# Linear attention ahead of an MLP: other feature layout, denominators from extra feature columns, smaller matmul tiles

## The chip, the cores and the metric

The kernel runs on one core of one Trainium2 chip. The metric is the device time of one execution in microseconds. A core has TensorE (PE, matmuls; its weight loads are shown apart as PEld), VectorE (DVE), ScalarE (ACT), GpSimd (POOL) and SyncE (SP), each with its own instruction queue, and 16 DMA engines. Matmuls write to PSUM, which has 8 banks of 512 fp32 columns in 128 partitions; only VectorE and ScalarE read it for the others.

## The reference

Inputs are q, k, v of shape (4 batches, 4 heads, 1088 tokens, 32), S1 and S2 of shape (8, 32), and the MLP's w_in (128, 2048), w_out (2048, 128), alpha (2048).

```
phi(x)  = outer(S1 x, S2 x), 8 x 8 = 64 features per token and head
kv      = sum over tokens of phi(k) v^T;   z = sum over tokens of phi(k)
attn    = (phi(q) kv) / (phi(q) . z + 1e-6)
x       = attn with the 4 heads side by side: (4 * 1088 = 4352 tokens, 128)
h       = x w_in
out     = (max(h, 0) + alpha * min(h, 0)) w_out
```

Everything comes in and leaves in fp32; the MLP runs in bf16, attention in fp32.

## The kernel before, in words

**MLP.** max(h,0) + alpha min(h,0) is (1 - alpha) relu(h) + alpha h. So the MLP is relu(x w_in) times w_a = (1 - alpha) w_out, plus x times W = w_in (alpha w_out). `w_b_f`, `w_hl` (its high and low bf16 halves) and `winT` serve to form W once (L598). Tokens go through in groups of 512 (`mlp`, L942): 16 matmuls h (L954), 16 ReLUs on ScalarE or VectorE into bf16 (`rh`, L960 and L962), 17 accumulating matmuls (L975; L972 in the last, short group), a 32x32 block transpose on VectorE (L982) and a store. There are 8.5 groups; the last batch's second half is three groups of 256: the rest tokens, 256 tokens, 256 tokens.

**Keys.** `kfeat` and `keys`: a batch has 1024 main tokens, 8 a partition, and 64 "rest" tokens that are loaded, featured and summed apart (`k_rest`). Keys are transposed, multiplied with S1 and S2 (L636), copied from PSUM (L361), and their 64 products formed by VectorE or GpSimd (L653). k'v (L706, rest L726) and z (L719, rest L733) are small fp32 matmuls; two more (L757, L766) bring them into the form that the queries need.

**Queries.** `queries` and `ratio` keep features in partitions (64 per pair of token halves) and tokens in columns. Two rounds of eight 32x64-tile matmuls give S1 q and S2 q, each repeated to 64 rows (L828; L872 for batch 0, which comes in two halves); ScalarE copies one, VectorE multiplies it with the other (L842). Eight 64x32-tile matmuls give the denominators, repeated over 32 rows, eight more the numerators (both L785). The denominators are transposed (L792), get EPS added (L798), are inverted (L799), spread by a second transpose (L801), and multiplied into the numerators (L807), which gives x in bf16. The rest tokens of all batches take the same way once (`q_rest`).

**Order.** No loop sets the order. `plan` is a list scheduler over all operations: each has engines that it may run on, a duration, latencies, a due time worked back from the MLP's pace (`T0`, `TG`) and shifted by the table `SHIFT`; PSUM banks and SBUF buffers (`classes`) are given out as it goes. It yields one fixed sequence per engine. `FIRST` holds its due times for the first loads. SP issues all loads of q, k, v and the weights in program order, then the stores; GpSimd has the key products and most of the weight work (L556). Ahead of the first group TensorE also runs matmuls without use (`dummy`, L499) to stay busy.

Of the kernel before, what the change touches and what calls it, by code (L numbers as in the profile page):

```python
# [11 lines left out]
F32 = mybir.dt.float32  # L12
# [22 lines left out]
class Op:  # L35
# [245 lines left out]
def kernel(  # L281
# [54 lines left out]

    def sb(b):
        return tiles[b.cls][b.slot]

    PK_MOST, PQ_MOST, PH_MOST = 3, 6, 4  # L340
    AW = 64
    KPE = [True, False, False, False]
# [724 lines left out]
```

## Time and profile before

| | |
|---|---|
| median of 3 runs | 113.41 us (113.07 to 113.61) |
| span of the profiled execution, first to last instruction | 110.9 us |
| between the two | 2.5 us |
| PE / PEld busy | 105.3 / 54.9 us |
| DVE / ACT / POOL busy | 83.7 / 75.5 / 24.1 us |
| DMA | 11.25 MB, mean 101 GB/s |
| first MLP matmul, last matmul ends | 15.39 us, 107.6 us |

The profile states no total of its own for the profiled execution; its span is set beside the median of the runs. Each view counts in microseconds from the span's start. "Busy" for a matmul includes its modelled pipeline, so busy times of matmuls that overlap add up to more than the clock. A row of the chain of waits is: start, length, what ran. A row in the order of time is: start, length, engine, line of the code, operation, output <- inputs, shapes, count, and in brackets the idle time before it with what ended it. A row of a group has busy time and mean length after the first bar, idle time behind the second.

### The profile page before, as it was taken

The numbers are of one execution on the slowest core, as the hardware profiler recorded it, in microseconds if no ns is written. First come the engines' busy times: TensorE is split into PE (matmuls) and PEld (weight loads), VectorE is DVE, ScalarE is ACT, GpSimd is POOL, SyncE is SP. The second block draws the span as 40 slices with busy tenths as digits, with TensorE's granted clock in tenths as the row PEclk, the third lists the DMA queues.
The fourth block names the chain that finished last, engine by engine and source line by source line (L and its number), as shares of the span: only waits on it lengthen the run. The fifth ranks groups of instructions, "written<-read, shape, count | busy, mean of one in ns | idle before, by whom it ended". The sixth has DMA issues, their size and how long they took to land.

```text
span 110.9 us, 3535 instructions
## 1 busy us (share of the span) xinstructions
PE 105.3 (95%) x1458; PEld 54.9 (50%) x1458; DVE 83.7 (75%) x157; ACT 75.5 (68%) x161; POOL 24.1 (22%) x24
## 2 busy tenths in 40 slices
PE   7999989989999989999999999999999999999980
PEld 2677333626354653447443353444534544588870
DVE  3179879999989388995667978986538798679850
ACT  2444699987689671891983963597596278797860
POOL 2040099980039008921500000000000000000000
PEclk9999999999999999999999999999999999999999
DMA  2999999779669942041002200050050005033231
GB/s 76 267 284 298 243 310 312 154 198 315 101 145 343 145 68 46 6 71 29 0 0 47 47 6 0 6 95 0 0 87 8 6 0 95 0 57 56 33 59 48
DMA packets 37536, 11.25 MB, mean 101 GB/s; under 512 B 27008, under 2 KB 37520, under 8 KB 37520
## 3 DMA queue, kind: packets, MB, share of 16 engines
q1 hardware_dynamic: 37264, 10.95, 41.9%
q8 instruction: 11, 0.18, 0.7%
q10 hardware_dynamic: 256, 0.08, 0.3%
q14 instruction: 5, 0.04, 0.2%
HBM read 8.80 MB, written 2.23 MB: 99 GB/s over the span
## 4 chain that ended last, share of the span: by engine, by line
PE 75%; SPq 8%; DMA 6%; POOL 5%; issue 2%; DVE 1%; ACT 0%; DVEq 0%
PE ps L975 26%; PE ps L954 24%; SPq L385 8%; PE ps L785 7%; PE ps L828 6%; DMA w_out_f<-in_moe_w_out_dram 6%; PE ps L636 3%; PE ps L706 3%; POOL w_b_f L556 2%; POOL w_a_bf L556 2%; PE ps L972 2%; PE ps L598 2%; POOL w_hl L556 1%; PE ps L757 1%; PE ps L726 1%
## 5 line engine op out<-in xcount | busy, mean ns | idle before, releaser
L954 PEld LDWEIGHTS <-w_in_bf 128*128 128x128 bf16 x160 | 15.0, 98 | 15.4 <-issue 3.6
L954 PE MATMUL ps<-xT__96,w_in_bf 128*128 128x512 bf16 (+1 forms) x80 | 21.5, 358 | 0.4 <-ACT rh__82 L960 0.4
L975 PEld LDWEIGHTS <-w_a_bf 128*128 128x128 bf16 x144 | 13.6, 98 | 14.4 <-issue 2.0
L954 PE MATMUL ps<-xT__97,w_in_bf 128*128 128x512 bf16 (+1 forms) x80 | 19.2, 336 | 0.0
L960 ACT ACTIVATE rh__82<-ps 128x512 bf16<-128x512 f32 (+1 forms) x22 | 12.2, 555 | 4.9 <-PE ps L954 4.7
L960 ACT ACTIVATE rh__83<-ps 128x512 bf16<-128x512 f32 (+1 forms) x22 | 11.9, 543 | 3.6 <-PE ps L954 3.6
L960 ACT ACTIVATE rh__84<-ps 128x512 bf16<-128x512 f32 (+1 forms) x16 | 8.5, 532 | 0.9 <-PE ps L954 0.6
L960 ACT ACTIVATE rh__86<-ps 128x512 bf16<-128x512 f32 (+1 forms) x15 | 8.3, 551 | 1.0 <-PE ps L975 0.5
L792 DVE STREAM_TRANSPOSE dt__78<-ps 128x1024 f32<-128x1024 f32 (+2 forms) x6 | 5.6, 937 | 3.9 <-PE ps L785 3.9
L975 PE MATMUL ps<-rh__83,w_a_bf 128*128 128x512 bf16 (+1 forms) x22 | 7.9, 359 | 0.0
L960 ACT ACTIVATE rh__85<-ps 128x512 bf16<-128x512 f32 x11 | 6.7, 605 | 0.9 <-PE ps L954 0.9
L975 PE MATMUL ps<-rh__82,w_a_bf 128*128 128x512 bf16 (+1 forms) x20 | 7.3, 363 | 0.0
L960 ACT ACTIVATE rh__87<-ps 128x512 bf16<-128x512 f32 (+1 forms) x11 | 5.8, 527 | 2.0 <-PE ps L954 1.8
L975 PE MATMUL ps<-rh__84,w_a_bf 128*128 128x512 bf16 (+1 forms) x19 | 6.8, 357 | 0.4 <-POOL w_a_bf L556 0.4
L975 PE MATMUL ps<-rh__86,w_a_bf 128*128 128x512 bf16 (+1 forms) x20 | 7.1, 353 | 0.0
L975 PE MATMUL ps<-rh__85,w_a_bf 128*128 128x512 bf16 (+1 forms) x19 | 6.8, 356 | 0.0
L828 PE MATMUL ps<-qT__74,Sab 32*64 32x512 f32 x96 | 6.7, 613 | 0.0
L982 DVE STREAM_TRANSPOSE oT__91<-ps 128x512 f32<-128x512 f32 (+1 forms) x8 | 5.4, 681 | 1.6 <-PE ps L975 1.4
L962 DVE TENSOR_SCALAR rh__85<-ps 128x256 bf16<-128x256 f32 (+1 forms) x10 | 5.3, 527 | 1.7 <-PE ps L954 1.0
L653 POOL TENSOR_TENSOR kp__70<-ab__68 128x1024 f32<-128x1024 f32 x2 | 3.9, 1952 | 9.9 <-ACT ab__68 L361 5.3
L975 PE MATMUL ps<-rh__87,w_a_bf 128*128 128x512 bf16 (+1 forms) x17 | 6.0, 355 | 0.0
L653 POOL TENSOR_TENSOR kp__70<-ab__67 128x512 f32<-128x512 f32 (+1 forms) x2 | 3.0, 1510 | 13.6 <-ACT ab__67 L361 13.6
(158 smaller groups left out, 218.9 us busy)
## 6 DMA issues: line engine op xcount, KB each, us to landing
out_dram<-oT__91 SPq DMA_DIRECT2D x28, 64.0 KB, 1.9
k<-in_k_dram SPq DMA_DIRECT2D x3, 512.0 KB, 4.7
q<-in_q_dram SPq DMA_DIRECT2D x3, 512.0 KB
v<-in_v_dram SPq DMA_DIRECT2D x12, 128.0 KB, 5.6
w_in_f<-in_moe_w_in_dram SPq DMA_DIRECT2D x2, 512.0 KB, 7.2
w_out_f<-in_moe_w_out_dram SPq DMA_DIRECT2D x2, 512.0 KB, 7.1
k<-in_k_dram SPq DMA_DIRECT2D x2, 256.0 KB, 3.0
q<-in_q_dram SPq DMA_DIRECT2D x2, 256.0 KB, 3.4
```

The source lines that it names most:

```text
L385: (nc.sync if eng == "sp" else nc.scalar).dma_start(dst, src)
L556: return lambda e: (nc.vector if e == "dve" else nc.gpsimd).tensor_tensor(out=out, in0=a, in1=b, op=what)
L636: nc.tensor.matmul(ps(bf)[lo + i:lo + i + aw, j * 64:(j + 1) * 64], sb(bT)[:, j * cnt + i:j * cnt + i + aw], S12blk.rearrange("p h c -> p ...
L653: (nc.vector if e == "dve" else nc.gpsimd).tensor_tensor(out=dst, in0=i0, in1=i1, op=ALU.mult)
L785: nc.tensor.matmul(dst, w, mv, start=True, stop=True, skip_group_check=True)
L792: nc.vector.transpose(bview(sb(dt), [[1, nn]]).rearrange("p (c n) -> p c n", c=2), ps(bd)[:, :, :ncp])
L828: nc.tensor.matmul(ps(bufs[t // 2])[64 * c:64 * c + 64, t % 2, :nf], bview(Sab[32 * t:32 * t + 32, i], [[1, R]]), moving(sb(bq), t, c), st ...
L954: nc.tensor.matmul(ps(b)[:, :n], w_in_bf[:, c * 128:(c + 1) * 128], xs(), start=True, stop=True)
L960: nc.scalar.activation(sb(br)[:, :n], ps(b)[:, :n], ACTF.Relu)
L962: nc.vector.tensor_scalar_max(sb(br)[:, :n], ps(b)[:, :n], 0.0)
L975: nc.tensor.matmul(ps(bo)[:, :n], w, y(), start=c == 0, stop=c == NC)
L982: o = op("dve", dv(n) + 40, lambda e: nc.vector.transpose(bview(sb(boT), [[1, n]]), ps(bo)[:, :n]), [last], [bo, boT], 80, end, f"oT{g}")
```

## The change

It rewrites attention's data layout and leaves the MLP as it is.

- **Tokens.** A partition now holds 34 tokens of one head (128 partitions are 4 heads x 32), so one contiguous row per partition is loaded for k and q. All 1088 tokens go one way; the loads, features and sums of the "rest" are gone. Token slots in a 32-column block are split over four column groups of 8 or 9; two of the 34 slots of each batch (64 tokens) go to a small tensor `xr`, which makes up the group of 256 that the rest tokens made up before.
- **Keys** (`key_part`). One block transpose (L604 of the new file), 8 matmuls on 64x32 tiles with S1 and S2 (L610), a transpose back (L613), products (L626) on GpSimd (VectorE helps for batch 0), k'v (L665, L670) and z (L650, L656).
- **Denominator weights.** z, as an 8x8 matrix, is masked (L679), multiplied with S1 (L682) and reduced into 8 more columns of the query weight `Wq` of its batch (L685): the denominator of a token is the dot product of S2 q with these 8 columns.
- **Queries** (`query_part`). Sixteen matmuls on 32x32 tiles (L711) give 24 features per token and head; VectorE transposes them (L717), forms the denominator as 8 products and a sum with EPS (L724, L725), inverts it (L730) and multiplies S2 q by it (L731). Then come the 64 products (L742; VectorE or GpSimd), their transposes (L745), and 32 matmuls on 32x32 tiles for the numerators (L756), which are x already; ScalarE or VectorE copies them into bf16.
- **Scheduler.** New `T0`, `TG`, `FIRST`, `SHIFT` and buffer counts. The second part of batch 0's q is now loaded after the first halves of w_in and w_out.
- **Stores** follow the new token order, again 128 B pieces, 512 B in the last.

The core of the diff (the scheduler's table and the removed functions are left out):

```diff
-    T0, TG = 14500.0, 10200.0
+    T0, TG = 13000.0, 9200.0
...
+    def load_rows(name, t, src, b, lo=0, hi=NT):
+        load(name, "sp", t[b][:, lo * D:hi * D],
+             bass.AP(tensor=src.tensor, offset=b * H * S * D + lo * D, ap=[[NT * D, 128], [1, (hi - lo) * D]]),
+             128 * (hi - lo) * D * 4)
...
+        def fe(e):
+            for hp in range(2):
+                for c in range(4):
+                    P = slice(64 * hp, 64 * hp + 64)
+                    nc.tensor.matmul(ps(pair)[32 * c:32 * c + 32, hp, :n], Wk[P].rearrange("p a b c -> p (a b c)"),
+                                     sb(bT)[P, offs[c] * D:offs[c] * D + n], start=True, stop=True, skip_group_check=True)
+        o = op("pe", n * 1.67 + 30, fe, [o, c_Wk], [bT, pair], 200, name=tag + "ab", mode=2, ni=32)
+        o = op("dve", dv(2 * n) + 35, lambda e: nc.vector.transpose(
+            at(sb(bab), 0, [[2 * r, 2 * ns], [n, 2], [1, 2 * r]]), ps(pair)[:, :, :n]), [o], [pair, bab], 80, name=tag + "abT")
...
+        o1 = op("pe", 150, lambda e: nc.tensor.matmul(ps(bz)[:, 64:96], S1sel.rearrange("p h d -> p (h d)"), sb(bt),
+                                                      start=True, stop=True, skip_group_check=True), [o1, c_sel], [bz, bt], 200,
+                name=f"zM{b}", mode=1, ni=4)
+        w_done[b] = op("dve", 110, lambda e: nc.vector.tensor_reduce(
+            out=Wq[:, b, 2 * r:3 * r], in_=at(ps(bz), 64, [[1, r], [r, 4]]), axis=AX.X, op=ALU.add), [o1, c_Wq], [bz], 80, name=f"zW{b}")
...
+        def fe(e):
+            for c in range(4):
+                for h in range(H):
+                    P = slice(32 * h, 32 * h + 32)
+                    nc.tensor.matmul(ps(f2[h // 2])[32 * c:32 * c + 32, h % 2, :n], Wq[P, b],
+                                     sb(bT)[P, offs[c] * D:offs[c] * D + n], start=True, stop=True)
+        o = op("pe", n * 1.67 + 40, fe, [o, c_Wq, w_done[b]], [bT] + f2, 200, name=tag + "f", mode=2, ni=64)
+        ot = []
+        for y in range(2):
+            def ft(e, y=y):
+                nc.vector.transpose(at(sb(bf)[:, 0], 2 * y * D, [[D, 2], [H * D, ns], [1, D]]),
+                                    ps(f2[y])[:, :, :n].rearrange("p h (s t) -> p h s t", t=D))
...
+        def den(e):
+            t = sb(bt)
+            nc.vector.tensor_mul(t[:, :m, :r], F(r, r), F(2 * r, r))
+            nc.vector.tensor_reduce(out=t[:, :m, r + 1], in_=t[:, :m, :r + 1], axis=AX.X, op=ALU.add)
...
+        def rec(e):
+            t = sb(bt)
+            nc.vector.reciprocal(t[:, :m, r + 2], t[:, :m, r + 1])
+            nc.vector.tensor_mul(F(r, r), F(r, r), at(t[:, 0], r + 2, [[12, m], [0, r]]))
...
+        def num(e):
+            for y in range(2):
+                for h in range(H):
+                    for c in range(4):
+                        P = slice(32 * c, 32 * c + 32)
+                        w = ns if c in extra else main
+                        nc.tensor.matmul(ps(n2[c // 2])[32 * h:32 * h + 32, c % 2, :w * D], kvW[b][P, y, h],
+                                         at(sb(bp)[P, 0], (2 * h + y) * D, [[2 * H * D, w], [1, D]]),
+                                         start=y == 0, stop=y == 1, skip_group_check=True)
...
-        x[b] = q_main(b, LATE) if b else q_first(LATE)
-    xr, bxr = q_rest(LATE)
+        keys(b, LATE)
+        x[b] = query_main(b) if b else query_first()
```

More of the change, by code (lines that the diff above doesn't have):

```diff
@@ L338, in sb, with at @@
         return tiles[b.cls][b.slot]
+    def at(t, x, free):
+        return bass.AP(tensor=t.tensor, offset=t.offset + x, ap=[list(t.ap[0])] + [list(d) for d in free])
     PK_MOST, PQ_MOST, PH_MOST = 3, 6, 4
-    AW = 64
-    KPE = [True, False, False, False]
     ops = []
@@ L398 @@
-    v_rs = [consts.tile([128, H, D], F32, tag=f"vr{m}", name=f"vr{m}") for m in range(2)]
-    q_rs = consts.tile([128, 2, H, D], F32, tag="qr", name="qr")
+    k_sb = [consts.tile([128, NT * D], F32, tag=f"k{b}", name=f"k{b}") for b in range(B)]
+    q_sb = [consts.tile([128, NT * D], F32, tag=f"q{b}", name=f"q{b}") for b in range(B)]
+    v_sb = [consts.tile([128, H, 9 if b else 10, D], F32, tag=f"v{b}", name=f"v{b}") for b in range(B)]
     w_in_f = consts.tile([DM, NC, 132], F32, tag="w_in_f")
@@ L458 @@
     for b in range(1, B):
[L459 to L460 removed]
+        load_rows(f"k{b}", k_sb, k, b)
+        load_rows(f"q{b}", q_sb, q, b)
         load_v(b)
[L462 to L469 removed]
     def got(name):
@@ L488, in zeros @@
         nc.vector.memset(tab, 0.0)
-    op("dve", 950, zeros, due=-1e7, name="zero")
+        nc.vector.memset(Wq, 0.0)
+        for t in tiles["tm"]:
+            nc.vector.memset(t[:, :, r:r + 1], EPS)
+    op("dve", 1150, zeros, due=-1e7, name="zero")
     c_zero = ops[-1]
@@ L658 @@
-    rest_k, rest_ab = {}, {}
-    def k_rest(m, due, i=None):
-        rows = None if i is None else (SR * i, SR)
-        P = slice(0, 128) if i is None else slice(SR * i, SR * i + SR)
-        tag = f"kr{m}" if i is None else f"kr{m}.{i}"
-        o = kfeat([k_rs[m][P].rearrange("p h d -> p (h d)")], got(tag), due,
-                  lambda: bview(ab_rest[m], [[1, 64]]), lambda: bview(kp_rest[m], [[1, 256]]),
-                  [], [], ("dve",), tag, rows=rows)
-        for b in (2 * m, 2 * m + 1) if i is None else (2 * m + i,):
-            rest_ab[b] = o[0].deps[0]
-            rest_k[b] = o + got(tag.replace("k", "v", 1))
@@ L846, in q_first, with key_part, pr @@
-    def q_first(due):
+    kvW = [consts.tile([128, 2, H, D], F32, tag=f"kvW{b}", name=f"kvW{b}") for b in range(B)]
+    kv_done = [None] * B
+    w_done = [None] * B
+    def key_part(tag, src, needs, nj, offs, ns, kp_eng, split):
+        n = ns * D
+        bT, pair, bab = Buf("kT"), pq(), Buf("ab")
+        o = op("dve", dv(nj * D) + 35, lambda e: nc.vector.transpose(sb(bT)[:, :nj * D], src), needs, [bT], 80, name=tag + "T")
+        def fe(e):
[7 more added lines that the diff above has]
+            at(sb(bab), 0, [[2 * r, 2 * ns], [n, 2], [1, 2 * r]]), ps(pair)[:, :, :n]), [o], [pair, bab], 80, name=tag + "abT")
+        if split:
+            bkp, base = [Buf("kp"), Buf("kp")], (0, 0)
+        else:
+            bkp, base = [Buf("kp")] * 2, (0, 2 * ns)
+        res = []
+        for hp in range(2):
+            def pr(e, hp=hp):
+                m = 2 * ns
+                dst = at(sb(bkp[hp]), base[hp] * R, [[R, m], [r, r], [1, r]])
+                i0 = at(sb(bab), hp * m * r, [[r, m], [1, r], [0, r]])
+                i1 = at(sb(bab), n + hp * m * r, [[r, m], [0, r], [1, r]])
+                (nc.vector if e == "dve" else nc.gpsimd).tensor_tensor(out=dst, in0=i0, in1=i1, op=ALU.mult)
+            res.append(op(kp_eng[hp], {"dve": dv(128 * ns), "pool": 110 + 128 * ns * 1.8}, pr, [o],
+                          [bab, bkp[hp]], 80, name=f"{tag}kp{hp}"))
+        return bab, n, bkp, base, o, res
@@ new lines, in half, with f @@
+            def half(y, u=u):
+                def f(e, n2):
+                    x0, step = (32, 480) if u and y == 0 else (0, 512)
+                    copy(e, sb(bx)[:, u, 256 * y:256 * y + 256].rearrange("p (c n) -> p c n", c=2),
+                         at(ps(n2[y]), x0, [[step, 2], [1, 128]]))
+                    if u:
+                        copy(e, sb(br)[:, 0, y], at(ps(n2[y]), 640 * y, [[1, D]]))
+                return (f"x{u}.{y}", (256, 32) if u else (256,), [y], [bx, br] if u else [bx], f)
@@ L918, in q_rest, with half, f @@
-    def q_rest(due):
-        bx = Buf("xT")
-        def moving(qT, t, c):
-            w = qT[32 * t:32 * t + 32].rearrange("p h j d -> p (h j d)")
-            return w[:, 128 * c:128 * c + 128]
-        def nums(a, dst):
-            for be in range(2):
-                for h in range(H):
-                    for c in range(2):
-                        yield (2 * c + be, h, c, a[64 * c:64 * c + 64, 2 * be:2 * be + 2, 32 * h:32 * h + 32],
-                               dst(h)[:, c, 64 * be:64 * be + 64])
-        def xmul(g, num, rr):
-            yield bview(sb(bx), [[1, 1024]])[:, 128 * g:128 * g + 128], num[:, g, :128], rr[:, g]
-        aq, mu = queries("qr", got("qr0") + got("qr1"), due, q_rs.rearrange("p c h d -> p (c h d)"), 128, moving)
-        return ratio("qr", aq, mu, list(range(B)), nums, 128, xmul, bx, [0, 1]), bx
+        def half(g):
+            def f(e, n2):
+                copy(e, sb(bx)[:, g].rearrange("p (c n) -> p c n", c=2), at(ps(n2[g]), 32 * g, [[512 - 32 * g, 2], [1, 256]]))
+                if g:
+                    copy(e, sb(br)[:, b], at(ps(n2[1]), 0, [[768, 2], [1, D]]))
+            return (f"x{g}", (512, 64) if g else (512,), [g], [bx, br] if g else [bx], f)
@@ new lines, in turned, with f @@
+        def turned(c):
+            def f(e, n2):
+                if c == 0:
+                    copy(e, sb(br)[:, b], at(ps(n2[1]), 0, [[768, 2], [1, D]]))
+                    copy(e, sb(bx)[:, 1, :256], ps(n2[1])[:, 0, 32:288])
+                else:
+                    copy(e, sb(bx)[:, 1, 256:].rearrange("p (t s) -> p t s", s=8), ps(n2[1])[:, 1, :256].rearrange("p (s t) -> p t s", s=8))
+            return (f"x1.{c}", (256,) if c else (64, 256), [1], [bx] if c else [bx, br], f)
+        xc = [half(0)] + ([half(1)] if b < B - 1 else [turned(0), turned(1)])
```

499 lines of the change are left out of this document (161 added, 338 removed), and 201 rows, old and new, of the table SHIFT.

## The prediction

> **What bounds the kernel now.** I read the page's first two parts for the engine that is always busy, then the chain of waits for the point from which nothing else matters, then the order in time for prices.
>
> ```profile
> span 110.9 us, 3535 instructions
> PE 105.3 (95%) x1458; PEld 54.9 (50%) x1458; DVE 83.7 (75%) x157; ACT 75.5 (68%) x161; POOL 24.1 (22%) x24
> PE   7999989989999989999999999999999999999980
> PEclk9999999999999999999999999999999999999999
> PE 75%; SPq 8%; DMA 6%; POOL 5%; issue 2%; DVE 1%; ACT 0%; DVEq 0%
> ```
>
> TensorE has work in every slice, at the full granted clock throughout, and is three quarters of the chain of waits. The chain in order of time shows where it takes over:
>
> ```profile
> 10.53 6.56 DMA w_out_f<-in_moe_w_out_dram
> 17.16 2.04 POOL w_b_f L556 x2
> 19.19 1.00 POOL w_a_bf L556
> 21.27 1.16 POOL w_hl L556
> 23.48 0.82 PE ps L975 x3
> 24.30 1.04 PE ps L828 x16
> 25.35 0.59 PE ps L785 x16
> 26.26 1.75 PE ps L598 x16
> 28.01 0.43 PE ps L954 x2
> 36.45 1.03 PE ps L706 x64
> 37.48 0.12 PE ps L719 x16
> 38.96 0.11 PE ps L626
> 63.17 1.07 PE ps L785 x16
> 106.37 1.24 PE ps L972 x22
> 107.63 0.30 DVE oT__93 L363
> ```
>
> Up to 23.5 us the chain runs over the second half of w_out (landed at 17.09) and the weight work on GpSimd. From there to 107.6 it is TensorE alone; after it come 110.9 - 107.6 = 3.3 us of copy and store. So this kernel's time is a head, a TensorE stream, and 3.3 us. The stream's first MLP matmul:
>
> ```profile
> 15.39 0.82 PE L954 MATMUL ps<-xT__96,w_in_bf 128*128 128x512 bf16 x3
> ```
>
> From 15.39 to 107.6 are 92.2 us. The MLP is 8.5 groups of 512 tokens with 33 matmuls each; two take 0.43 us, so 280.5 x 0.2155 = 60.4 us. The bf16 product of the two weights (L598) is 1.75. What is left, 30 us, is attention (with the weight transposes and under 1 us of idle). That is the part the change rewrites.
>
> **The stream after.** I list what the changed kernel puts on TensorE behind its first MLP matmul, in its own order: feature work of batches 1 to 3, and the last product of batch 0's second half. Prices are the rows above. Eight fp32 tiles with one matmul each (16 records of L785; an fp32 matmul leaves two) take 0.59 us at 256 columns and 1.07 at 512, so 1.875 ns a column and 0.11 fixed: 0.65 at 288, 0.62 at 272, 0.38 at 144.
> - Key features: 8 matmuls on 64x32 tiles, 288 columns: 0.65 x 3 = 1.95.
> - Query features with denominators: 16 matmuls on 32x32 tiles, 288 columns. If sixteen run as eight do, 0.65 x 3 = 1.95.
> - Numerators: 32 matmuls in two rounds of sixteen, on average 272 columns: 1.24 x 3 = 3.72; the half of batch 0 has 144 columns: 0.76.
> - k'v: 32 + 4 matmuls, 72 records at 1.03 / 64 = 16.1 ns: 1.16 x 3 = 3.48.
> - z: 10 matmuls, 20 records at 0.12 / 16: 0.15 x 3 = 0.45; its product with S1, taken as 0.1: 0.3; two transposes of 0.11 (the L626 row): 0.66.
>
> Together 13.3 us instead of 30. All of before's denominators, second feature product, rest keys and the rest query path are gone from the stream. With 60.4 and 1.75 unchanged the stream is 75.5 us, 16.7 less than the 92.2.
>
> **What nobody has run yet is sixteen tiles at once.** The trace has at most eight (32x64 and 64x32). The bounds are 16 at a time (6.43 us for query features and numerators) and 8 (twice that, +6.4). I take sixteen: the rows below are 32-row tiles in all four row groups, and the L706 row above has 32-column tiles in all four column groups, and both overlap.
>
> ```profile
> 24.23 1.11 PE L828 MATMUL ps<-qT__74,Sab 32*64 32x512 f32 x16
> L828 PE MATMUL ps<-qT__74,Sab x96: 587/613/639, 24.2 to 67.9; 32*64 32x512 f32 x96
> ```
>
> Sixteen records of 613 ns, 9.8 us in all, pass in 1.04 us of the chain. The Trainium skill (TensorE: Matmul & The Clock Gate, "Measured speedup vs the span model") gives 10.6 times for sixteen bf16 tiles; counted as 10.6 tiles in place of 16 that would be an estimate of 6.43 x (16/10.6 - 1) = 3.3 us more. No row here has sixteen.
>
> **The head.** GpSimd keeps ten weight operations: four on w_out's first half, then six behind the second half's landing. Before:
>
> ```profile
> 13.88 1.04 POOL L556 TENSOR_TENSOR w_b_f<-w_out_f,alphaT 128x512 f32<-128x512 f32 x1 [5.47 <-DMA w_out_f<-in_moe_w_out_dram]
> 15.87 1.16 POOL L556 TENSOR_TENSOR w_hl<-w_b_f,w_hl 128x512 bf16<-128x512 f32 x1
> 23.39 1.03 POOL L556 TENSOR_TENSOR w_b_f<-w_out_f,alphaT 128x512 f32<-128x512 f32 x1
> L653 POOL TENSOR_TENSOR kp__71<-ab__68 128x1024 f32<-128x1024 f32 x1 | 2.0, 1955 | 0.0
> ```
>
> About the same bytes go ahead of w_out's second half (3.7 MB), so I keep its 17.1; two w_b, one w_a and three w_hl after it are 2.04 + 1.00 + 3 x 1.16 = 6.5, which gives 23.7. The first half may land up to 0.9 us earlier than before (13.88), since the second q part of batch 0 is now queued behind it; if not, its four operations end at 18.0 and the six at 24.5. I take 23.9. Behind them in GpSimd's queue now stand batch 1's two key products of 1152 elements: 1152/1024 x 1.955 = 2.2 each, until 28.3. TensorE's order has batch 1's k'v, then batch 0's second numerators, ahead of the second MLP group, so it waits there: before that point it has 24 MLP matmuls, the weight product and small work, 8.5 us from its first MLP matmul. That first one needs: q0.1 landed (2.72 MB ahead and with it, as many as w_out's first half had, so 12.9 to 13.9), its transpose, the transpose of the first products, numerators, two feature transposes of q0.1 and a copy, all in VectorE's order: 0.67 + 1.15 + 0.8 + 0.6 + 0.33 and waits, 16.2 to 17.4. The sixteen first ReLUs, mostly on ScalarE at 0.49 a start, hold it until about 24; then 1.75 + 0.65 bring TensorE to 26.5. So 28.3 decides, with 1.8 us of slack for the first matmul. k'v with its wait to 29.6, numerators to 30.3. Of the 75.5, 5.2 + 0.65 + 0.15 + 0.1 + 1.75 + 0.65 + 1.16 + 0.76 = 10.4 have passed; 65.1 are left.
>
> **The other engines.** They decide whether TensorE stays fed. Starts of consecutive operations give their pace:
>
> ```profile
> 60.75 1.23 DVE L815 STREAM_TRANSPOSE qT__74<-q 128x1024 f32<-128x1024 f32 x1
> 61.91 1.18 DVE L842 TENSOR_TENSOR aq__76<-ps,aq__76 128x1024 f32<-128x1024 f32 x1
> 64.35 1.25 DVE L792 STREAM_TRANSPOSE dt__78<-ps 128x1024 f32<-128x1024 f32 x1 [0.65 <-PE ps L785]
> 65.63 0.21 DVE L798 TENSOR_SCALAR dt__78<-dt__78 128x32 f32<-128x32 f32 x1
> 65.87 0.36 DVE L799 RECIPROCAL dt__78<-dt__78 128x32 f32<-128x32 f32 x1
> 66.26 1.25 DVE L801 STREAM_TRANSPOSE rr__80<-dt__78 128x1024 f32<-128x1024 f32 x1
> L681 DVE STREAM_TRANSPOSE kT__64<-k x2: 611/620/630, 27.1 to 27.6; 128x256 f32<-128x256 f32 x2
> 20.20 0.60 ACT L960 ACTIVATE rh__85<-ps 128x512 bf16<-128x512 f32 x1
> 20.69 0.60 ACT L960 ACTIVATE rh__82<-ps 128x512 bf16<-128x512 f32 x1
> ```
>
> 1024 elements cost VectorE 1.16, and 0.12 more where the next operation needs them. Per batch it did: key transposes 4 x 0.55, q 1.16, two products 2.3, dT 1.28, add and reciprocal 0.6, rr 1.39, x 1.2: 10.1, with 0.8 for z. After: k and q transposes 1.2 each, ab 0.67, features 2 x 0.67, denominators 0.85, reciprocal and division 0.8, products 2.55 where VectorE has them (batch 2; one of two in batch 3, none in batch 1), their transposes 2.55, z 0.3: 8.9 to 11.5. So VectorE gets nothing off while the stream gets 17 us shorter. ScalarE loses two copies of 0.96 and its ab copies and gains two x copies of 0.5: about 1.4 less a batch. Until batch 1's numerators VectorE has about 18 us of work against a stream of 20 plus its waits, in the next two stages 14.3 against 21.6 and 14.4 against 14.5, so it runs ahead before the tight one. I take 1.5 us for waits in the rest: three group starts where only 0.86 to 1.08 us of other matmuls cover the copy of x (0.2 + 0.6 + 0.07), and some late ReLUs. Bounds: 0, and 4 from the second rival.
>
> **Loads and stores.** The loads of q, k, v and weights are still issued by SP; k and q rows grow from 1 KB to 4.3 KB, v rows from 256 B to 1 KB. From b = 1 on loads lie behind 60 us of stream and I give them nothing. Stores keep 128 B pieces, and the last store 512 B, so the 3.3 us tail stays.
>
> **Sum.** 30.3 + 65.1 + 1.5 = 96.9 for the last matmul, + 3.3 = 100.2 span. The median of the runs is 113.41 beside a span of 110.9; the 2.5 between them I keep: 102.7 us.
>
> **Rivals.**
> 1. Sixteen tiles run as more than eight but fewer than sixteen: 102.7 to 109.1. For it: no row shows sixteen. Against: both halves of the pattern overlap fully. The Trainium skill's figure (same section) gives 106.0, an estimate.
> 2. VectorE feeds TensorE late. L681 writes its result with a stride and pays 0.55 us for 256 elements, twice the plain price; the new ab and feature transposes write rearranged too. If they cost double, 3 x 0.57 = 1.7 us more a batch, and up to 2 more where ReLUs queue behind; 104 to 107. Against: they write whole runs of 16 or 32.
> 3. The GpSimd wait isn't there, since w_out lands earlier or the products are covered: 16.2 + 75.5 + 1.0 + 3.3 + 2.5 = 98.5.
> 4. Small records have a floor of their own, so that more tiles at once don't help. There are 96 + 256 + 48 + 216 + 60 + 6 + 12 = 694 behind the first MLP matmul; at L706's 16.1 ns they take 11.2 us, under the 13.3, and nothing changes. The Trainium skill (TensorE: Matmul & The Clock Gate, "Wait — 56ns, not 53.3ns?") has starts never under about 25 ns apart: by that rule 17.4 us, 106.8 in all, an estimate; L706's 64 records in 1.03 us disagree.
> 5. Slower: the tiles' overlap breaks down, as only one column or row group streams at a time. At w tiles at a time, query features and numerators cost 6.43 x 16/w; w = 4 gives +19.3, 122 us. It decides below w = 6, where 6.43 x (16/6 - 1) = 10.7 eats the whole gain. Against: eight overlap in L785 and L828.
>
> **How the numbers follow.** Forecast 0.60 (100 to 105 by itself); rival 1, 0.12; 2, 0.09; 3, 0.08; 4, 0.02; 5, 0.07; no measurable change (within 0.5%, about what a measurement of this kernel can tell), 0.02. That is 0.91 faster, 0.02 same, 0.07 slower. The range from 98.5 (rival 3) to 108.5 leaves out rival 5, no change, and the edges of 1 and 3, under 2 in 10.
>
> **What would show it.** Right: TensorE's attention lines behind its first MLP matmul near 13 us; 16 numerators' rounds in about 0.6 us; one idle stretch of 1 to 3 us before batch 1's k'v, ended by GpSimd; VectorE over 80% busy; the tail 3.3. Wrong: numerators near 2.4 us a batch (rival 1), TensorE idle before VectorE lines all through (2), no idle at k'v (3).

## The result and the profile after

The changed kernel takes 109.84 us, the median of four executions (107.89 to 113.08), beside 113.42 for the kernel before. The ratio is 0.959 (95% interval 0.949 to 0.969); it leaves out executions that the comparison takes for disturbed, while the medians in this document are over all. So it is faster, as forecast, but by about 4% and not by 9.5%, and 109.84 lies above the range. The profiled execution took 109.28 us: a span of 107.5 and 1.8 around it.

The page's first two parts and its chain by engine, of the kernel after:

```profile
span 107.5 us, 3290 instructions
PE 96.5 (90%) x1351; PEld 52.0 (48%) x1365; DVE 81.5 (76%) x139; ACT 72.0 (67%) x157; POOL 40.1 (37%) x30
PE   7968897796969989999999899999999999999950
DMA  2999999999998123001400140041023014051131
PE 57%; POOL 11%; DVE 10%; ACT 6%; DMA 5%; issue 4%; SPq 3%; DVEq 0%
```

TensorE is busy for eight tenths or more of every slice from the thirteenth (32 us) to the last two, as before, but the first third now has gaps, and TensorE's share of the chain fell from 75% to 57%: the head has grown, and other engines set it. While it lasts, the DMA engines are full (the 9s of the last row but one, up to 32 us). The chain in order of time:

```profile
20.58 2.28 POOL w_hl L543 x2
22.86 2.25 POOL w_a_bf L543
25.11 1.12 POOL w_hl L543
26.23 2.14 POOL kp__68 L626
28.36 2.15 POOL kp__69 L626
30.55 0.97 PE ps L665 x51
31.52 0.83 issue
33.02 1.10 PE ps L756 x37
34.28 1.03 PE ps L842 x4
42.86 1.51 PE ps L756 x41
66.81 1.70 PE ps L756 x44
```

GpSimd ends its key products at 30.5, batch 1's k'v (L665) follows at once, breaks off after 51 of its records, and goes on 0.83 us later. Batch 0's second numerators (L756) end at 34.12 and the MLP resumes at 34.28. (Those 0.16 us are most likely one MLP matmul without a record: this trace lists 1365 weight loads but only 1351 matmuls, and in the control below, with 1365 of both, the same stretch is five matmuls in 1.19 us without a gap, where here 0.16 is followed by four in 1.03. I keep 34.28.) The forecast had 30.3 for that point, 96.9 for the last matmul and 100.2 for the span; the trace has 34.28, 103.7 and 107.5. Of the 7.3 us that the span is too long, 4.0 lie ahead of that point, 2.8 behind it, and 0.5 in the tail.

### The profile page after: what moved, and what is told of

The parts are those of the page before. It is cut to its first block, busy times and chain, and to the rows that moved or that the text cites. A ratio compares the mean times of both kernels' runs of the same rounds, so it can differ in the third digit from the quotient of the medians.

```text
span 107.5 us, 3290 instructions
## 1 busy us (share of the span) xinstructions
PE 96.5 (90%) x1351; PEld 52.0 (48%) x1365; DVE 81.5 (76%) x139; ACT 72.0 (67%) x157; POOL 40.1 (37%) x30
## 4 chain that ended last, share of the span: by engine, by line
PE 57%; POOL 11%; DVE 10%; ACT 6%; DMA 5%; issue 4%; SPq 3%; DVEq 0%
PE ps L842 21%; PE ps L821 21%; PE ps L756 6%; DMA v<-in_v_dram 5%; POOL w_hl L543 3%; SPq L386 3%; POOL w_a_bf L543 2%; POOL kp__69 L626 2%; POOL kp__68 L626 2%; POOL w_b_f L543 2%; PE ps L665 2%; PE ps L711 2%; PE ps L839 2%; DVE ft__73 L731 2%; DVE ph__75 L742 1%
## 5 line engine op out<-in xcount | busy, mean ns | idle before, releaser
L821 PE MATMUL ps<-xT__94,w_in_bf 128*128 128x512 bf16 (+1 forms) x80 | 19.8, 337 | 0.3 <-DVE Wq L685 0.3
L821 PE MATMUL ps<-xT__93,w_in_bf 128*128 128x512 bf16 x62 | 19.0, 379 | 0.9 <-ACT xT__93 L365 0.5
L827 ACT ACTIVATE rh__81<-ps 128x512 bf16<-128x512 f32 (+1 forms) x22 | 12.2, 556 | 4.9 <-PE ps L821 4.8
L626 POOL TENSOR_TENSOR kp__68<-ab__66 128x1152 f32<-128x1152 f32 (+1 forms) x5 | 9.7, 1955 | 13.5 <-DVE ab__66 L613 12.9
L827 ACT ACTIVATE rh__82<-ps 128x512 bf16<-128x512 f32 (+1 forms) x20 | 11.3, 567 | 0.9 <-PE ps L821 0.8
L742 POOL TENSOR_TENSOR ph__76<-ft__73 128x1280 f32<-128x1280 f32 (+1 forms) x2 | 5.6, 2822 | 15.6 <-DVE ft__73 L731 15.6
L827 ACT ACTIVATE rh__83<-ps 128x512 bf16<-128x512 f32 (+1 forms) x18 | 9.8, 544 | 2.1 <-PE ps L656 1.0
L482 PE MATMUL ps<-const-bfloat16-1.0 128*128 128x512 bf16 x27 | 8.5, 448 | 1.1 <-PEq L911 0.8
L842 PE MATMUL ps<-rh__82,w_a_bf 128*128 128x512 bf16 (+1 forms) x22 | 7.9, 359 | 0.5 <-issue 0.5
L717 DVE STREAM_TRANSPOSE ft__73<-ps 128x576 f32<-128x576 f32 (+2 forms) x10 | 6.0, 642 | 2.7 <-PE ps L711 2.7
L827 ACT ACTIVATE rh__84<-ps 128x512 bf16<-128x512 f32 (+1 forms) x14 | 7.4, 529 | 0.9 <-PE ps L821 0.8
L827 ACT ACTIVATE rh__85<-ps 128x512 bf16<-128x512 f32 (+1 forms) x12 | 7.1, 593 | 0.2
L756 PE MATMUL ps<-pt__77,kvW 32*32 32x128 f32 (+3 forms) x320 | 7.2, 353 | 0.0
L745 DVE STREAM_TRANSPOSE pt__77<-ph__75 128x1280 f32<-128x1280 f32 (+1 forms) x5 | 6.9, 1383 | 0.1
L827 ACT ACTIVATE rh__86<-ps 128x512 bf16<-128x512 f32 (+1 forms) x10 | 5.4, 539 | 2.0 <-PE ps L821 2.0
L827 ACT ACTIVATE rh__87<-ps 128x512 bf16<-128x512 f32 (+1 forms) x12 | 6.4, 532 | 0.5 <-PE ps L821 0.2
L842 PE MATMUL ps<-rh__81,w_a_bf 128*128 128x512 bf16 (+1 forms) x19 | 6.7, 351 | 0.0
L742 DVE TENSOR_TENSOR ph__75<-ft__73 128x1280 f32<-128x1280 f32 (+1 forms) x4 | 6.6, 1640 | 0.1
```

What stands on the lines that cost most here:

```text
L482: nc.tensor.matmul(PS[:, 7], ones(128), ones(512), start=True, stop=True, skip_group_check=True)
L626: (nc.vector if e == "dve" else nc.gpsimd).tensor_tensor(out=dst, in0=i0, in1=i1, op=ALU.mult)
L717: nc.vector.transpose(at(sb(bf)[:, 0], 2 * y * D, [[D, 2], [H * D, ns], [1, D]]), ps(f2[y])[:, :, :n].rearrange("p h (s t) -> p h s t", t=D))
L742: (nc.vector if e == "dve" else nc.gpsimd).tensor_tensor(out=dst, in0=i0, in1=i1, op=ALU.mult)
L745: oT.append(op("dve", dv(k) + 35, lambda e, lo=lo, hi=hi, bph=bph: nc.vector.transpose(sb(bp)[:, lo:hi].rearrange("p a b -> p (a b)"), sb( ...
L756: nc.tensor.matmul(ps(n2[c // 2])[32 * h:32 * h + 32, c % 2, :w * D], kvW[b][P, y, h], at(sb(bp)[P, 0], (2 * h + y) * D, [[2 * H * D, w], ...
```

## The experiments

The point at which TensorE resumes the MLP behind batch 0's second numerators splits every trace below into a head and a rest. I call it the resumption.

### Single operations measured alone

A kernel of its own, without the computation: VectorE's forms alone and beside GpSimd, then rounds of small fp32 matmuls.

```diff
+ for n, f, t in ((1024, dve_ss, "ss"), (288, dve_ss, "sm"), (1024, dve_sd, "sd"), ...):   # alone
+     f(n, t); f(n, t)
+ ...
+ for i in range(m): f(n, t)            # and, at the same time,
+ for i in range(4): pool_ss(512, t)
+ ...
+ for n in (32, 64, 128, 160, 208, 256, 288, 512):        # 2 rounds on 16 tiles: 64 records
+     for y in range(2): for h in range(4): for c in range(4):
+         nc.tensor.matmul(PS[32*h:32*h+32, 2+c, :n], w[32c..], mv[32c.., 512*y:512*y+n], start=y==0, stop=y==1)
```

> This kernel leaves the whole computation out (it writes zeros) and measures single operations. Part one: GpSimd's product of 512 elements and six VectorE forms, each alone and then beside the other engine. Theory (the two engines hinder each other when both read two operands from SBUF): GpSimd 1.03 us alone and 2.0 to 2.3 beside VectorE's products with two SBUF operands; VectorE's 1024-element product 1.2 alone and 1.9 to 2.4 beside GpSimd, its 288-element product 0.46 to 1.4; nothing changes beside a product that reads PSUM, a transpose, a sum or a ReLU. Rival (the long ones of the trace come from the loads that land at that time): with no loads here, no form gets longer. Part two: rounds of 64 records on 32x32 tiles with 32 to 512 columns. Theory (records have a floor of about 16.3 ns and sixteen tiles overlap fully beyond it): 1.04 us at 32, 64 and 128 columns, 1.19 at 288, 2.0 at 512. Rival (sixteen tiles run as about thirteen): 1.04, 1.45 at 288, 2.4 at 512. Rival (eight at a time): 2.2 at 288, 3.9 at 512.

Groups of VectorE alone (dss and dsm: both operands in SBUF; dsd: one in PSUM), and GpSimd alone; mean ns behind the comma:

```profile
L63 DVE TENSOR_TENSOR dss<-za,zb 128x1024 f32<-128x1024 f32 x2 | 2.4, 1222 | 0.0
L67 DVE TENSOR_TENSOR dsd<-ps,zb 128x1024 f32<-128x1024 f32 x2 | 2.4, 1221 | 0.0
L63 DVE TENSOR_TENSOR dsm<-za,zb 128x288 f32<-128x288 f32 x2 | 0.9, 456 | 0.0
L83 POOL TENSOR_TENSOR galone<-pa,pb 128x512 f32<-128x512 f32 x3 | 3.8, 1261 | 0.2
```

The same groups with both engines at work:

```profile
L63 DVE TENSOR_TENSOR dss<-za,zb 128x1024 f32<-128x1024 f32 x5 | 10.0, 2006 | 0.1
L83 POOL TENSOR_TENSOR gss<-pa,pb 128x512 f32<-128x512 f32 x4 | 7.6, 1906 | 0.2
L63 DVE TENSOR_TENSOR dsm<-za,zb 128x288 f32<-128x288 f32 x5 | 6.2, 1239 | 0.1
L67 DVE TENSOR_TENSOR dsd<-ps,zb 128x1024 f32<-128x1024 f32 x5 | 6.1, 1223 | 0.1
L83 POOL TENSOR_TENSOR gsd<-pa,pb 128x512 f32<-128x512 f32 x4 | 5.1, 1266 | 0.2
```

Beside GpSimd, VectorE's 1024-element product grows from 1.22 to 2.01 us and its 288-element one from 0.46 to 1.24, and GpSimd's from 1.26 to 1.91 (alone it was to take the 1.03 of the kernel's rows; why it takes 1.26 here was not tried). With one operand in PSUM nothing changes, nor did it for transposes, sums and ReLUs. Since no loads land in these stretches, they are not the cause. The Trainium skill (SBUF — State Buffer, "Who interferes with whom") says that a VectorE instruction with two SBUF inputs contends with a GpSimd instruction that reads SBUF, and that the second to issue waits; these rows agree.

The rounds by their pace in the chain (L113 sixteen tiles, 64 records, at 128, 288 and 512 columns; L121 eight tiles, 32 records, at 288 and 512; L128 four tiles in one column, 16 records, at 288), all at the full clock:

```profile
72.56 1.00 PE ps L113 x56
81.27 1.53 PE ps L113 x63
83.78 2.28 PE ps L113 x62
91.96 1.13 PE ps L121 x32
94.07 1.88 PE ps L121 x32
98.47 1.10 PE ps L128 x16
```

Each set is two rounds. From 288 to 512 columns sixteen tiles take 0.75 us more, and eight also 0.75: 3.3 ns a column for both, so sixteen overlap as fully as eight. What differs is the fixed part: 1.53 - 288 x 0.00333 = 0.57 us for 64 records, against 0.17 for 32 and 0.14 for 16. None of the three theories had that: the first gave 1.19 us at 288 columns, "thirteen tiles" gave 1.45 and 2.4 and came closest by its sizes, but its reason (an incomplete overlap) is wrong. The Trainium skill's factor of 10.6 for sixteen tiles (TensorE: Matmul & The Clock Gate, "Measured speedup vs the span model"; the table does not name the data type) lies between what these rows give: set against 3.3 ns a column without a fixed part, sixteen tiles do the work of 16 x 0.96 / 1.53 = 10.0 at 288 columns and of 16 x 1.71 / 2.28 = 12.0 at 512. Its least distance of about 25 ns between starts ("Wait — 56ns, not 53.3ns?") is undercut if records are counted, 64 in 1.00 us at 128 columns or 15.6 ns each; by matmuls, of which each leaves two records, it is 31 ns, and no run here shows which of the two the figure is for.

### Order in the head: numerators first, key products first, both

In the trace TensorE has the transposes of w_in's second half (L576), which wait for its load and cast, ahead of batch 0's first numerators; and GpSimd's weight products run into VectorE's. Rows of the kernel after, in order of time:

```profile
13.11 1.22 DVE L742 TENSOR_TENSOR ph__75<-ft__73 128x1024 f32<-128x1024 f32 x1
13.17 2.06 POOL L543 TENSOR_TENSOR w_b_f<-w_out_f,alphaT 128x512 f32<-128x512 f32 x1 [1.93 <-DVE ft__73 L731]
15.19 1.03 POOL L543 TENSOR_TENSOR w_a_bf<-w_out_f,omaT 128x512 bf16<-128x512 f32 x1
17.64 0.92 PE L576 MATMUL ps<-identb,w_in_bf 128*128 128x128 bf16 x8 [0.47 <-ACT w_in_bf L365]
18.49 1.07 PE L756 MATMUL ps<-pt__77,kvW 32*32 32x128 f32 x64
20.04 1.47 PE L821 MATMUL ps<-xT__93,w_in_bf 128*128 128x512 bf16 x5 [0.49 <-ACT xT__93 L365]
21.86 2.35 DVE L742 TENSOR_TENSOR ph__75<-ft__73 128x1280 f32<-128x1280 f32 x1
22.82 2.29 POOL L543 TENSOR_TENSOR w_a_bf<-w_out_f,omaT 128x512 bf16<-128x512 f32 x1
```

The first two moves, and the next two, alone and together:

```diff
+ behind("winT1", "q0.0num", 0)      # numerators first
+ behind("winTc1", "q0.0x0.1")
+ behind("q0.1ph0", "k1abT")         # key products first
+ behind("w_a3", "k1kp0")
```

> Only TensorE's order is changed: the transposes of the input weights' second half, and their copy, go behind batch 0's first numerators, so that these and the first MLP group don't wait for that half's load and cast. Theory A (the span is set later, where batch 1's k'v waits for GpSimd's two key products): the first MLP matmul comes about 1.0 us earlier than at 20.0, k'v of batch 1 starts where it did, within 0.3 us, and the time is that of the changed kernel within 0.3 us. Theory B (the first MLP matmul sets what follows, through ScalarE's and VectorE's ReLUs): the time falls by 0.8 to 1.2 us against the changed kernel, to about 108.7 where that is at 109.7.

> Only the order on GpSimd and VectorE is changed: one weight product of GpSimd goes behind batch 1's first key product, and the product of batch 0's second query features goes behind the transpose of batch 1's key features on VectorE. Theory A (GpSimd's queue alone sets the start of batch 1's k'v): the two key products end at about 28.9 in place of 30.5 and the time falls by 1.3 to 1.6 us. Theory B (TensorE's own work, fed by the ReLUs, ends at 30.35 too, so that GpSimd is level with it): the time falls by 0 to 0.4 us, and a wait of TensorE for ReLUs or the weight product stands where that for GpSimd stood.

> Both reorderings together. If the two paths are level in the changed kernel, as the trace reads, each alone gives little and both together give 1.0 to 2.0 us more than the sum of the two alone leaves to see: 107.5 to 108.5 us. If GpSimd's queue alone decides, this equals the key-products-first kernel within 0.3 us; if the first MLP matmul alone decides, it equals the numerators-first kernel within 0.3 us.

| | first MLP matmul | k'v of batch 1 starts | resumption | span | median |
|---|---|---|---|---|---|
| after | 20.04 | 30.55 | 34.28 | 107.5 | 109.84 |
| numerators first | 19.27 | 31.04 | 33.49 | 106.5 | 110.94 |
| key products first | 20.41 | 30.82 | 33.49 | 106.9 | 110.48 |
| both | 21.26 | 32.88 | 35.55 | 108.6 | 110.41 |

None gains. Numerators first brought the first MLP matmul 0.8 us forward, but k'v came no earlier: ScalarE's copy of the moved transposes now delays its casts for GpSimd, which waits 1.0 us for them. Key products first did not end those products at 28.9: the first took 3.43 us instead of 2.17, because VectorE's moved product (2.37 us) now ran beside it. The two together were to give 107.5 to 108.5 and gave 110.41, with a median inside the spread of the others. In the profiled execution TensorE was also granted half its clock from 12 to 14 us, which I can't explain from the order, so that trace does not show what both moves would do at the full clock. Four kernels with different heads and the same median said that something else was in the way.

### The changed kernel again, and the weight product without its low half

```diff
- tt(w_b_f[:, s], w_out_f[:, s], al, ALU.mult)(e)
+ tt(w_hl[:, s, 0], w_out_f[:, s], al, ALU.mult)(e)          # straight to bf16; w_hi and w_lo go
- nc.tensor.matmul(ps(bw)[:, :2 * DM], winT[:, c], w_hl[:, c].rearrange("p y m -> p (y m)"), ...)
+ nc.tensor.matmul(ps(bw)[:, :DM], winT[:, c], w_hl[:, c, 0], ...)
```

> The changed kernel itself, unaltered, beside the reorderings below on one chip, since its executions differ by several us. Theory (what differs is when TensorE gets past batch 0's second numerators, which hangs on the landing of the loads; behind that point everything takes the same time): the span less the start of the MLP matmul behind those numerators (34.28 us of 107.5 before) is 73.0 to 73.4 us again, as in the three reordered traces (106.5 - 33.49, 106.9 - 33.49, 108.6 - 35.55), whatever the span. Rival (the stream itself varies): this difference moves by as much as the span does.

> The low half of the weight product is left out: GpSimd writes the scaled output weights straight to bf16, its four low-half subtractions and ScalarE's four casts go, and the weight product has 128 columns in place of 256. The order is that of the changed kernel. Theory A (GpSimd's queue sets the start of batch 1's k'v): GpSimd reaches the key products as soon as VectorE has batch 1's key features (24.9), both are done at about 29.2 instead of 30.5, and the time falls by 1.0 to 1.5 us. Theory B (TensorE's own path from its first MLP matmul at 20.0, paced by ScalarE, sets it): the three casts of 0.5 us between the ReLUs and 0.9 us of the weight product go, and the time falls by 1.4 to 2.4 us, with the first MLP matmul where it was. If both are level the fall is the smaller of the two, 1.0 to 1.5.

> As the one without the low half, and batch 0's first numerators ahead of the transposes of the input weights' second half on TensorE. Theory B (the first MLP matmul counts): another 0.7 to 1.0 us less than without the reordering, 2 to 3 us under the changed kernel. Theory A (GpSimd alone): no further gain, within 0.3 us.

> As the one without the low half, with both reorderings (numerators first on TensorE; on VectorE batch 1's key features ahead of the product of batch 0's second query features, on GpSimd the first key product ahead of the last weight product). Both paths are relieved at once: 3 to 4 us under the changed kernel, about 106, if the two paths are level; no better than the numerators-first form if only TensorE's path counts.

Medians: the changed kernel 110.49 (107.80 to 111.96), without the low half 110.25 (one execution at 190.8, unexplained), with numerators first 110.63, with both moves 110.50. The three expectations of a gain failed. Span less resumption was 107.9 - 34.62 = 73.3 for the changed kernel, as the theory of a constant rest had it. So time changes hands only in the head, and there the chains show the same thing at the same place. The kernel after, again:

```profile
27.80 2.15 POOL kp__69 L626
29.99 0.97 PE ps L665 x51
30.96 1.73 issue
32.69 0.42 PE ps L665 x13
34.62 1.03 PE ps L842 x4
```

Without the low half and with numerators first, where k'v starts when ScalarE's ReLUs let it:

```profile
28.29 0.50 ACT rh__88 L826
28.84 0.76 PE ps L710 x26
29.59 0.90 PE ps L664 x50
30.49 1.92 issue
34.35 1.03 PE ps L841 x4
```

TensorE breaks off after the 50th or 51st record of the same 64, and waits for nothing that the profile shows. How long does not hang on when k'v starts: 0.83 us after a start at 30.55, 1.73 after 29.99, 1.92 after 29.59, but 1.99 with both moves and no low half, where it started at 31.38. The queue called "instruction" moves blocks of 16 KB (0.16 MB in 10 packets). In the changed kernel's second trace one such packet appears in the stretch 30.0 to 30.2 us, 2.5 to 2.7 us ahead of the break's end; with numerators first and no low half in 29.8 to 30.0, 2.4 to 2.6 ahead. The five traces with a break all go on 2.4 to 3.1 us behind such a packet; the trace with numerators first alone has it at 26.8, long before k'v, and no break. The packet of the changed kernel's second trace, in the stretch 30.0 to 30.2 us:

```profile
q8 instruction: 1, 0.02, 33.1%
```

That suggested to me that TensorE runs out of instructions, whose block stands in line with the loads. That this queue is TensorE's is read from these times alone.

### The loads of later batches held back

```diff
+ hold("k3", k_sb[3][:, :1], "k1kp1")        # load k of batch 3 behind GpSimd's first key product of batch 1
+ hold("q3", q_sb[3][:, :1], "k1kp0")
+ hold("v2", v_sb[2][:, 0, 8, :1], "q1ph0")  # each by a one-column store of GpSimd into the tile
+ hold("v3", v_sb[3][:, 0, 8, :1], "q1ph1")
```

> The changed kernel, with four groups of loads held back: k and q of batch 3 until GpSimd's two key products of batch 1 are done, v of batches 2 and 3 until its two query products of batch 1 are done (a one-column store of GpSimd into the tile holds each back). Nothing else changes. Theory F (the break in the middle of batch 1's k'v, which the profile calls issue, is TensorE waiting for its next 16 KB block of instructions, whose packet is delayed by the loads): with the loads out of the way the block's packet lands before 28 us in place of 29.6 to 30.0, the break of 0.8 to 1.7 us is gone, and the median falls by 1 to 2 us, to 108.5 to 109.3; the executions spread less. Rival (the break is something of k'v's own, or the loads share nothing with it): packet, break and time stay within 0.3 us.

> The loads held back as before, and batch 0's first numerators ahead of the transposes of the input weights' second half on TensorE. Theory F: freed of the break, the earlier first MLP matmul now counts: 0.3 to 1.0 us less than with the held loads alone, 108.0 to 108.6. Rival: as the numerators-first kernel without held loads, 110.9.

> The loads held back, numerators first, and the low half of the weight product left out (GpSimd and ScalarE relieved by eight operations, the weight product by 0.9 us). Its twin without held loads broke off for 1.92 us in batch 1's k'v and resumed the MLP at 34.35. Theory F: resumes at 32.4, span 105.5, 107.3 us. Rival: 110.6 like its twin.

With the loads alone held back the median is 108.07 (ratio 0.958, 0.953 to 0.963), 1.8 to 2.4 us under the changed kernel's two medians, and five of six executions lie between 107.7 and 108.9. The ratio is no better than the changed kernel's 0.959, and the best executions are alike (107.72 here, 107.80 and 107.89 there): what changed is how often an execution comes near the best. Of executions with a granted clock of 0.99 or more, the eight of the changed kernel have spans of 105.8 to 110.0 us, the ten with the loads held back (with the control below) 105.7 to 107.1. Each run has one trace, and none of the changed kernel's best executions was profiled, so that they too break off, or don't, is not shown. The break is gone in all three traces. With numerators first the median is 110.16, a miss: GpSimd, which waits for ScalarE's casts there, ended its key products only at 33.55, in a trace that was granted half its clock from 14 to 16 us. Without the low half as well it is 108.73, not 107.3.

### The control, the query weights first, and both reliefs

```diff
+ behind("k0.1kp0", "zW0")     # VectorE: batch 0's key product behind the sum that completes the query weights
```

> The changed kernel with the loads of batches 2 and 3 held back, again, as the control for the next two on one chip: 108.1 us median, within 0.5 us.

> As the control, and VectorE's product of batch 0's keys (768 elements) goes behind the sum that completes batch 0's query weights. Theory P (that product takes 1.02 us or, beside GpSimd's, 2.09, and the query features of batch 0 wait for it in some executions, at 12.1 in place of 10.4): the features start near 10 us in every execution, the slow executions go, and the median falls by 0.3 to 1 us, to 107.1 to 107.8. Rival (the loads' landing decides the spread): no change within 0.3 us.

> As the one before, with the low half of the weight product left out (eight operations less on GpSimd and ScalarE, 0.9 us less on TensorE). If nothing else stands in the way of TensorE's path through the first sixteen ReLUs, 1.0 to 2.0 us less than the one before: 105.5 to 106.5. If it resumes the MLP at the same time (some other wait in its place), the same within 0.3 us.

The control repeats at 108.14 (ratio 0.954, 0.947 to 0.961). Its chain, without a break, and its packets of instructions in the stretch 26.4 to 26.6 us:

```profile
28.49 2.14 POOL kp__69 L626
30.69 1.10 PE ps L665 x64
33.14 1.19 PE ps L842 x5
```

```profile
q8 instruction: 1, 0.02, 43.2%
```

The stretch from 25 to 30 us, first in the changed kernel, then in this one (last three columns: TensorE's granted clock, the DMA engines' busy share, which this view can put a little over 1, and GB/s):

```profile
25.00:30.00 5.00, 4.79 (x78) 3.39 (x79) 4.89 (x7) 4.00 (x10) 5.00 (x4) 1.00 1.08 249
```

```profile
25.00:30.00 5.00, 4.86 (x66) 3.41 (x79) 4.84 (x7) 4.08 (x10) 5.00 (x5) 1.00 0.17 32
```

With the DMA engines at 0.17 of their time in place of 1.08 the block's packet is there 3 us earlier (26.4 against 29.6), and k'v passes 64 records in one run: from its start to the end of the numerators 2.45 us (30.69 to 33.14) instead of 3.57 (30.55 to 34.12). Full DMA engines don't always bring a break: of the eight traces with the loads running five have one, of the six with the loads held back none. But the block's packet comes 7.4 to 10.8 us behind the packet before it in the eight, and 3.4 to 6.0 in the six.

One rival is not excluded. The kernels were measured in groups, and no group has the changed kernel both with and without the loads held back. All five breaks lie in two groups, and those five traces also lack 14 matmul records each, where the other nine lack none; a group of three kernels without the loads held back (numerators first, key products first, both) has no break. So the breaks could go with the group, or with the recording, and not with the loads. The packet's distance, and the forecast that held for the loads alone, speak for the loads. And since those three reorderings have no break and still have medians of 110.4 to 110.9, the break is not all that makes executions long.

The Trainium skill (Runtime: NRT & Kernel Launch, "Instruction fetch mechanics") says that instructions come in 16 KiB blocks by a DMA queue of the sequencer's own, and that crossing a block is mostly hidden; the block size agrees with the packets, and the crossing was hidden in all six traces in which the loads left room, but in only three of the other eight.

Query weights first gave 108.23, no change: theory P fell. The features did start earlier (10.65 against 11.06 us), but VectorE's product took 2.0 us beside GpSimd's in both traces (2.00 and 2.08), and behind the sum it still stood in front of the features' transposes, which began no earlier (11.75 and 11.71).

Without the low half on top, the median is 107.07 (106.74 to 108.00), ratio 0.947 (0.940 to 0.953): the fastest here, under both kernels, with a weight product of one bf16 half instead of two. Its chain:

```profile
28.55 0.50 ACT rh__88 L826
29.09 0.76 PE ps L710 x26
29.85 1.03 PE ps L664 x64
32.23 1.19 PE ps L841 x5
```

The same relief that gave nothing in the median under the loads (110.25) gave 1.2 us with them held back; by the best executions it is 0.4 us there (107.38 against 107.80) and 0.9 here (106.74 against 107.66). The expectation was 105.5 to 106.5; now ScalarE's ReLUs decide when k'v starts. In all traces of this section with the clock at full in that part the rest, span less resumption, is 73.0 to 73.4 us (105.3 - 32.23 = 73.1 here, 106.5 - 33.14 = 73.4 in the control).

## Why the prediction was right or wrong

**Right in kind.** TensorE's stream bounds the kernel, it got shorter, and the kernel got faster; loads from batch 1 on cost nothing where their data is used. For each further column sixteen tiles cost what eight cost (3.3 ns for two rounds), so the overlap that I assumed is there, and rivals 1 and 5 fall by their mechanism; in size the numerators, at 1.51 us instead of 1.24, came out as rival 1 would have them at 13 of 16 tiles. Rival 3 is out too: GpSimd's products end the chain ahead of k'v, and later than forecast. Rival 2 (VectorE late) shows only in one short wait, at 61 us. From the first MLP matmul to the last matmul's end the trace has 103.7 - 20.04 = 83.7 us, against 92.2 before and 75.5 plus waits forecast.

**The step "until 28.3" (GpSimd), mis-sized by 2.2 us.** I priced ten weight operations by rows where GpSimd worked alone. In the changed kernel VectorE has its 64-feature products of batch 0, both operands in SBUF, at the same time: one operation took 2.06 us and another 2.29 instead of 1.03, together 2.3 us more, and the measurement of single operations, without loads, shows the same lengthening. The ten took 13.0 us, to 26.2 instead of 23.9. The rise of VectorE's own product to 2.35 (1.49 for the same 1280 elements later) belongs to it.

**The step "28.3 decides, with 1.8 us of slack for the first matmul", wrong.** The first MLP matmul came at 20.04, not by 17.4: I had left out that TensorE's order puts the transposes of w_in's second half ahead of batch 0's numerators, and the wait for v of batch 0. Moving the transposes brought 0.8 of the 2.6 us; how the rest splits was not tried. That used up the slack, and the two ways ended level, at 30.4 and 30.5. That would explain why moving one of them gave nothing, but moving both gave nothing either, so it is argued and not shown.

**The step "k'v with its wait to 29.6, numerators to 30.3", short by 1.8 us.** GpSimd to resumption took 3.8 us instead of 2.0. Of it 1.1 is the break for instructions (3.57 us against the control's 2.45 for the same work), in a mechanism that the prediction does not have at all: it gave the loads from batch 1 on nothing. In the second trace the break was 1.73 instead of 0.83, and holding the loads back won 1.8 to 2.4 us in the median, though nothing in the best executions. That the loads keep the block back is argued and not shown, since the breaks could also go with the group of measurements; so the cause of this part stays in part open. Of the rest 0.5 is the price of k'v and of the numerators, below, and 0.16 most likely the matmul without a record. The 4.0 us of the head are these steps: 2.2 + 1.8.

**The term "numerators 1.24 x 3", mis-sized by 1.0 us.** They took 1.51, 1.70 and 1.51. I had 0.11 us fixed and 1.875 ns a column for each round of tiles; measured are 0.57 fixed for 64 records and 3.3 ns for two rounds, 1.48 at 272 columns. Rival 4 (small records cost of their own) was given 2 in 100 and is the nearest to it, though by another rule than the one it named. By rival 4's price, 16.1 ns a record, the 64 records would take 1.03 us. The 1.70 of batch 2 stays unexplained.

**The rest of "65.1 left + 1.5 waits", short by 1.8 us.** z takes 0.41 instead of 0.15 (two batches, 0.5), k'v 1.28 instead of 1.16 (0.2), query features 0.70 instead of 0.65 (0.1), and nine returns from small tiles to the MLP cost 0.11 each (1.0): in the key-products-first trace, which has all its records, four MLP matmuls behind numerators take 0.97 us instead of 0.86. The waits were less than the 1.5: by the starts of the MLP matmuls 0.43 us is lost after 39.0, for ScalarE, and 0.43 at 61, for VectorE; five further gaps, each the length of one matmul, are missing records, since the key-products-first trace lacks them. That is 1.2 of the 1.8; the other 0.6 I can't place.

**The tail** was 3.8, not 3.3, and what lies around the span 1.8, not 2.5; they nearly cancel.

**What was to show it.** The attention lines behind the first MLP matmul come to about 16 us, not 13. The idle stretch before batch 1's k'v that GpSimd ends is 0.2 us, not 1 to 3, since TensorE itself was late. VectorE is busy 76%, not over 80%.

## What to carry to other kernels

An operation's price from a trace holds for its neighbours of that time: before giving a busy engine more work, look which of its instructions read two operands from SBUF and what the other engine that does so will be running beside them. Denser instruction streams need their code in time: where "issue" breaks a burst of matmuls always at the same instruction while loads fill the DMA engines, try holding back the loads that aren't due yet, and measure the kernel with and without that side by side; here the kernel with that change alone had a lower median than any with a reordering alone, because long executions were rarer. When several changes that each relieve a real wait leave the median where it was, look for a resource that none of them touched.

## What the runs showed of the hardware that I had not expected

- In five traces TensorE stopped for 0.8 to 2.0 us in the middle of a burst and went on 2.4 to 3.1 us behind a packet of instructions; with the later loads held back the packet came earlier and no trace has the stop. That the loads cause it is argued, not shown.
- Two rounds of small fp32 matmuls cost 3.3 ns a column however many of the 16 tiles are filled, and a fixed 0.14 us for 16 records, 0.17 for 32, 0.57 for 64.
- VectorE's 288-element product takes 0.46 us, and 1.24 beside GpSimd's products; its 1024-element product with one operand in PSUM is untouched (1.22 and 1.22).
- In some executions TensorE was granted half its clock for 2 to 4 us in the head, and whole executions at nearly full clock still differ by up to 4 us; with the loads held back that was 1.4 us in the control and its first run (spans 105.7 to 107.1), though one execution with the query weights first still took 108.8. What starts the drop of the clock was not tried.
